# Transposing layernorm outputs and residual gradients by DMA in a two-block training step on one core

## The chip, the cores and the metric

The kernel runs on one core of a Trainium2 chip. The metric is the device time of one execution in microseconds, as the median of several runs. The core has five engines that run their own streams of instructions: TensorE (PE in the profile: matmuls, with weight loads listed as PEld), VectorE (DVE), ScalarE (ACT), GpSimd (POOL) and SyncE (SP, which here only issues DMAs). Sixteen DMA engines move the data that the queues ask for. "SPq" in a view is SP's DMA queue.

## What is computed

A forward and backward pass through four residual layers over one sequence of 2048 rows by 512 columns: linear attention (A), gated unit (B), A, B again, with the same weights in both rounds. The outputs are the result, the gradient of the input, and the gradients of the five weights.

```python
def _A_ref(x, wqkv, wo):            # 32 heads of 16
    q, k, v = ...(x @ wqkv)
    phi = lambda t: jnp.where(t > 0, t + 1, jnp.exp(t)) + 1e-6
    pq, pk = phi(q), phi(k)
    kv = jnp.einsum("bhsd,bhse->bhde", pk, v)
    z = jnp.einsum("bhsd->bhd", pk)
    o = einsum(pq, kv) / (einsum(pq, z) + 1e-6)
    return o @ wo

def _B_ref(x, w_gate, w_up, w_down):   # 512 -> 1376 -> 512
    return (sigmoid(x @ w_gate) * (x @ w_up)) @ w_down

x = x + _A_ref(_layernorm(x), A_wqkv, A_wo)
x = x + _B_ref(_layernorm(x), B_w_gate, B_w_up, B_w_down)
...                                 # both once more, then jax.vjp of all of it
```

## The kernel before, in words

The 2048 rows are 16 tiles of 128 rows (`NST`); the residual stream stays in SBUF for the whole kernel as 16 tiles `x` of 128x512 in float32. In the forward pass it holds the activations, in the backward pass the gradients. A 128x512 tile is four blocks of 128x128 (`NDC`), since a matmul sums over 128 partitions.

A scheduler orders the instructions of each engine when the program is built. It starts from the order of the source and may hoist an instruction whose inputs it thinks are ready. On each engine the order is then fixed, and every instruction waits for what it needs. All DMAs but those of the last stage are issued from SP's queue, in order. Each of them also waits for the DMA issued eight places earlier on that queue, because eight completion semaphores are used in turn.

Stages, in order of time:

- **Forward of A** (`a_fwd`, layers 0 and 2). Loop 1 takes each tile through q, k, v: three groups of four 128x512 matmuls (L468), exponentials on ACT, the rest on DVE, then a transpose of the positive feature map. Loop 2 (L521 to L546) forms the attention output and adds it to `x`. In layers 0 and 2 the transposes of the weights for the backward pass (L372, L396; one PSUM buffer for all) are emitted at tile 4 of loop 1; the scheduler spreads them.
- **Forward of B** (`b_fwd`, layers 1 and 3). Per tile 24 matmuls for gate and up (L621, L624), transposes of their product (L587), 11 matmuls for down (L599).
- **First backward pass of each layer** (`b_bwd_p1`, `a_bwd_p1`), layers 3, 2, 1, 0: from the gradient tile in `x` to the gradient of the layer's input. It saves what the weight gradients need to DRAM.
- **Second backward pass** (`b_bwd_p2`, `a_bwd_p2`): weight gradients, matmuls over all 16 tiles (L833, L863, L885), partly placed between the first passes by the scheduler.

The places that the change touches:

*Layernorm tiles in the forward pass.* Class `FwdLN` prepares one tile at a time. `stage` normalizes `x[st]` into a bf16 slice of `hstage` (statistics on DVE, power on POOL, scaling on ACT at L310), saves four tiles at once to DRAM (L426), and makes `hT`, the four transposed blocks, which the matmuls of L468, L621 and L624 use as weights. `hT` is made by `transpose_blocks`: four TensorE transposes into a PSUM tile `ln_tp` (L318), then one copy to SBUF on DVE (L325). `ensure(st + 1)` at L460 and L609 keeps it one tile ahead. The first `NPRE` = 2 tiles of the next layer are prepared at the end of the layer before (L547, L602).

*Gradient tiles in the first backward passes.* Class `GPrep`, `prep(st)`: in layer 3 the gradient is loaded from the input into `gstage` and copied to `x` (L669, L671); in the other layers `x[st]` is cast to bf16 into `gstage` on POOL (L676) and saved, two tiles at a time (L678). Then `gT`, its four transposed blocks, is made in the same way through the PSUM tile `gT_ps`, with the copy on ACT (L327). It feeds L760 in layers 3 and 1, and L958 in layers 2 and 0. `prep` is called at the top of each tile's work (L749, L948). Beside it stand the loads of what the forward pass saved: `ssd`, `h`, `o`, `pq` (L751, L696).

At the start of the kernel SP loads the input and the weights in the order x, `wqkv`, `wo`, `wg`, `wu`, `wd` (L98 to L168), with the last of x in between.

## Time and profile before

| | |
|---|---|
| median of 3 timed runs | 1394.78 us (1393.33 to 1395.5) |
| profiled execution: span from first to last instruction | 1393.1 us |
| mean granted TensorE clock | 0.988 |
| q/k/v loops (first to last L468) | 19.7 to 309.9 us, layers 0 and 2 |
| gate/up (first to last L621) | 114.8 to 475.9 us, layers 1 and 3 |
| first backward pass, B (first to last L760) | 489.5 to 1018.6 us, layers 3 and 1 |
| first backward pass, A (first to last L958) | 650.2 to 1131.4 us, layers 2 and 0 |
| end of the span | weight gradients alone |

The profile is of one execution; its page lists no other time of that execution than the span. Of the engines it lists the time in which they were busy. Matmuls are pipelined and the ends of their intervals are modelled, so the price of a matmul in a full stream is read from the starts of two neighbours and not from its listed length. In a table of stages each row is a stretch of the span with each engine's busy time. In a line of a group, the number after the first bar is the busy time of all its instructions and the mean of one in ns; after the second bar stands the engine's idle time just before them and what ended it.

### The profile page before, as it was taken

Reading aid. Unit: us, or ns where it says so; the run is one execution under the profiler, and the core shown is the slowest. Engines: PE = TensorE matmul, PEld = TensorE weight load, DVE = VectorE, ACT = ScalarE, POOL = GpSimd, SP = SyncE. Lnnn points to the kernel's source line nnn. Section 1 sums busy time; section 2 is a strip of 40 time slices with the busy share of each in tenths; the row PEclk is TensorE's granted clock in tenths of the full one; section 3 lists DMA queues with packets and bytes.
Section 4 is the critical chain, followed back from the end, with each engine's and each line's share of the span. In section 5 each row is a group of like instructions: output and inputs, shape, how many; then the busy total and the mean of one; then the engine's idle time right before and its main releaser. Section 6 shows DMA issues by size and latency. Waiting matters only on the chain. (4 is left out here: it accounts for less than half of the span.)

```text
span 1393.1 us, 25045 instructions
## 1 busy us (share of the span) xinstructions
PE 1297.9 (93%) x9956; PEld 790.1 (57%) x9956; DVE 679.9 (49%) x1468; ACT 647.3 (46%) x1168; POOL 250.5 (18%) x413
## 2 busy tenths in 40 slices
PE   4989899998899898998999999999999999988988
PEld 2555455556455444554665677555548675556767
DVE  6664644567533355665857400456640676611111
ACT  5857576775776544443547411444431447600000
POOL 4026654105633300002100100010010101100000
PEclk9999999999999999999999999999999999999999
DMA  7622334452543497547774586964568956499745
GB/s 273 230 103 103 149 152 158 147 177 98 201 178 143 169 326 259 175 168 237 218 230 148 181 227 149 334 217 167 172 199 248 275 169 192 143 311 261 175 122 162
DMA packets 268853, 269.77 MB, mean 194 GB/s; under 512 B 24576, under 2 KB 245184, under 8 KB 268736
## 3 DMA queue, kind: packets, MB, share of 16 engines
q1 hardware_dynamic: 246272, 253.50, 57.2%
q10 hardware_dynamic: 22464, 14.68, 3.6%
q8 instruction: 78, 1.28, 0.4%
q14 instruction: 39, 0.32, 0.1%
HBM read 144.57 MB, written 123.57 MB: 192 GB/s over the span
## 5 line engine op out<-in xcount | busy, mean ns | idle before, releaser
L730 ACT COPY ddT<-T_ps 128x1024 bf16<-128x1024 bf16 (+1 forms) x96 | 83.1, 867 | 103.4 <-PE T_ps L728 103.3
L630 POOL TENSOR_TENSOR ssd_t<-hh_t,oms 128x512 bf16<-128x512 bf16 (+1 forms) x96 | 100.6, 1052 | 83.0 <-ACT oms L628 48.4
L648 DVE SCALAR_TENSOR_TENSOR junk<-t_sb,h_ld 128x512 bf16<-128x512 f32 x64 | 46.1, 720 | 137.6 <-ACT t_sb L646 136.6
L762 DVE TENSOR_TENSOR dd_t<-dhh_ps,ssd_ld 128x512 bf16<-128x512 f32 (+1 forms) x96 | 60.4, 629 | 102.0 <-PE dhh_ps L760 102.0
L742 PEld LDWEIGHTS <-ddT 128*128 128x128 bf16 (+1 forms) x704 | 66.3, 98 | 71.4 <-issue 12.5
L468 PE MATMUL mm_ps<-wqkv,hT 128*128 128x512 bf16 x384 | 100.2, 386 | 0.5 <-DVE x_108 L601 0.4
L742 PE MATMUL dh_ps<-wuT,ddT 128*128 128x512 bf16 (+1 forms) x352 | 96.5, 382 | 3.9 <-ACT t_sb L646 0.9
L833 PE MATMUL p_ps<-p_set,p_a_15354 128*128 128x256 bf16 (+1 forms) x768 | 82.5, 267 | 10.8 <-DVE dw_stg L798 10.8
L629 DVE TENSOR_TENSOR hh_t<-u_ps,ssd_t 128x512 bf16<-128x512 f32 (+1 forms) x96 | 60.7, 634 | 65.3 <-PE u_ps L624 50.3
L760 PE MATMUL dhh_ps<-wdT,gT 128*128 128x512 bf16 (+1 forms) x384 | 87.8, 364 | 5.0 <-DMA wdT<-wdT_d 4.3
L624 PE MATMUL u_ps<-wu,hT 128*128 128x512 bf16 (+1 forms) x384 | 92.4, 361 | 0.0
L621 PE MATMUL g_ps<-wg,hT 128*128 128x512 bf16 (+1 forms) x384 | 92.0, 361 | 0.4 <-DVE ostage L530 0.4
L833 PE MATMUL p_ps<-p_set,p_a_10151 128*128 128x256 bf16 (+1 forms) x768 | 81.5, 261 | 0.9 <-DMA p_set<-sv_hdd_130 0.9
L599 PE MATMUL y_ps<-wd,hhT 128*128 128x512 bf16 (+1 forms) x352 | 81.4, 380 | 0.0
L742 PE MATMUL dh_ps<-wgT,ddT 128*128 128x512 bf16 (+1 forms) x352 | 81.3, 379 | 0.0
L833 PEld LDWEIGHTS <-p_a_15354 128*128 128x128 bf16 x768 | 68.9, 100 | 21.7 <-issue 8.4
L590 ACT COPY hhT<-hhT_ps 128x512 bf16<-128x512 bf16 (+1 forms) x96 | 49.5, 515 | 58.3 <-PE hhT_ps L587 58.1
L728 PEld LDWEIGHTS <-dd_t 128*128 128x128 bf16 (+1 forms) x704 | 50.7, 101 | 40.8 <-DVE dd_t L762 18.5
L833 PEld LDWEIGHTS <-p_a_10151 128*128 128x128 bf16 x768 | 67.2, 98 | 9.2
L728 PE MATMUL T_ps<-ident,dd_t 128*128 128x128 bf16 (+1 forms) x704 | 66.4, 221 | 3.6 <-DVE dd_t L762 3.5
L838 DVE TENSOR_TENSOR dw_stg<-p_ps,dw_stg 128x512 bf16<-128x512 f32 (+1 forms) x36 | 23.4, 653 | 87.5 <-PE p_ps L833 74.4
L1038 PE MATMUL dh_ps<-wqkvT,dkvT 128*128 128x512 bf16 x256 | 65.6, 380 | 0.0
(493 smaller groups left out, 2498.3 us busy)
## 6 DMA issues: line engine op xcount, KB each, us to landing
p_set<-sv_hdd_130 SPq DMA_DIRECT2D x15, 1024.0 KB, 7.1
p_set<-sv_hdd_119 SPq DMA_DIRECT2D x15, 1024.0 KB, 6.3
sv_ssd_118<-ssd_t SPq DMA_DIRECT2D x16, 688.0 KB, 3.1
sv_ssd_129<-ssd_t SPq DMA_DIRECT2D x16, 688.0 KB, 3.1
ssd_ld<-sv_ssd_129 SPq DMA_DIRECT2D x16, 688.0 KB, 5.5
sv_hdd_130<-dd_t SPq DMA_DIRECT2D x16, 688.0 KB, 3.9
ssd_ld<-sv_ssd_118 SPq DMA_DIRECT2D x16, 688.0 KB, 6.0
sv_hdd_119<-dd_t SPq DMA_DIRECT2D x16, 688.0 KB, 3.7
```

The costliest lines, as they stand in the source:

```text
L468: nc.tensor.matmul(ps[:], lhsT=hT[:, kc, :], rhs=k.wqkv[:, kc, n * D:(n + 1) * D], start=(kc == 0), stop=(kc == NDC - 1))
L599: nc.tensor.matmul(y_ps[:], lhsT=T["hhT"][0:r, fc, :], rhs=k.wd[0:r, fc, :], start=(fc == 0), stop=(fc == NFC - 1))
L621: nc.tensor.matmul(g_ps[:, 0:w], lhsT=hT[:, kc, :], rhs=k.wg[:, kc, c0:c0 + w], start=(kc == 0), stop=(kc == NDC - 1))
L624: nc.tensor.matmul(u_ps[:, 0:w], lhsT=hT[:, kc, :], rhs=k.wu[:, kc, c0:c0 + w], start=(kc == 0), stop=(kc == NDC - 1))
L629: nc.vector.tensor_tensor(hh_t[:, c0:c0 + w], u_ps[:, 0:w], ssd_t[:, 0, c0:c0 + w], ALU.mult)
L630: nc.gpsimd.tensor_tensor(ssd_t[:, 1, c0:c0 + w], hh_t[:, c0:c0 + w], oms[:, 0:w], ALU.mult)
L728: nc.tensor.transpose(tps[0:r, a, i, :], dd[:, a, fc * P:fc * P + r], k.ident[:])
L730: nc.scalar.copy(ddT[:, :, fcs[0]:fcs[0] + nfull, :], tps[:, :, 0:nfull, :])
L742: nc.tensor.matmul(dh_ps[:], lhsT=T["ddT"][0:r, a, fc, :], rhs=wT[0:r, fc, :], start=(i == 0), stop=(i == n_mm - 1))
L760: nc.tensor.matmul(dhh_ps[:, 0:w], lhsT=gT[:, jc, :], rhs=k.wdT[:, jc, c0:c0 + w], start=(jc == 0), stop=(jc == NDC - 1))
L833: nc.tensor.matmul(psv[:, icl, :], lhsT=lhs_all[:, st, ic * P:(ic + 1) * P], rhs=set_t[:, st, 0:W], start=(st == 0), stop=(st == NST - 1))
L1038: nc.tensor.matmul(dh_ps[:], lhsT=lhsT, rhs=k.wqkvT[:, n * NDC + c, :], start=(i == 0), stop=(i == 3 * NDC - 1))
```

## The change

Both uses of `transpose_blocks` in the two classes are replaced by a DMA that transposes from SBUF to SBUF, issued on SP's queue. The PSUM tiles `ln_tp` and `gT_ps` and the copies that empty them are no longer used there. `hT` gets 7 buffers in place of 4, `gT` 4 in place of 2. Layernorm tiles are prepared three tiles ahead in place of one, and 4 in place of 2 at the end of the layer before. Gradient tiles, so far prepared when they were needed, are prepared two tiles ahead by a new method `get`. All other transposes stay on TensorE.

```diff
-                hT=lctx.enter_context(tc.tile_pool(name="ln_hT", bufs=4)),
+                hT=lctx.enter_context(tc.tile_pool(name="ln_hT", bufs=7)),
...
-NPRE = 2
+NPRE = 4
...
         hT = R["hT"].tile([P, NDC, P], BF16, name="hT")
-        transpose_blocks(k, R["ps"], hT[:], [h_t[:, c * P:(c + 1) * P] for c in range(NDC)], "vector", tag="ln_tp")
+        nc.sync.dma_start_transpose(out=hT[:], in_=h_t)
...
-                ln.ensure(st + 1)
+                ln.ensure(st + 3)
...
-            ln.ensure(st + 1)
+            ln.ensure(st + 3)
...
+        self.done, self.ready = 0, {}
...
-        gT = self.work.tile([P, NDC, P], BF16, name="gT")
-        transpose_blocks(k, self.ps_tp, gT[:], [g_bf[:, c * P:(c + 1) * P] for c in range(NDC)], "scalar",
-                         tag="gT_ps")
+        gT = self.stg.tile([P, NDC, P], BF16, name="gT", bufs=4)
+        nc.sync.dma_start_transpose(out=gT[:], in_=g_bf)
         return g_bf, gT
+
+    def get(self, st):
+        while self.done <= min(st + 2, NST - 1):
+            self.ready[self.done] = self.prep(self.done)
+            self.done += 1
+        return self.ready.pop(st)
...
-            g_bf, gT = gp.prep(st)
+            g_bf, gT = gp.get(st)
...
-                g_bf, gT = gp.prep(st)
+                g_bf, gT = gp.get(st)
```

In the compiled program PE's stream begins with nine groups of four weight transposes (L372 on `wg`), and the first L468 follows them; before, it began with the transposes of two layernorm tiles and then L468. On SP's queue the first transposing DMAs stand right behind the loads of the weights. In the text below, line numbers are those of the kernel before; in the changed kernel the transposing DMAs are at L428 (hT) and L681 (gT).

## The prediction

> **What bounds the kernel now.** I read the page's busy times first, then the busy slices, then the table of stages, and last single groups.
>
> ```profile
> span 1393.1 us, 25045 instructions
> ...
> PE 1297.9 (93%) x9956; PEld 790.1 (57%) x9956; DVE 679.9 (49%) x1468; ACT 647.3 (46%) x1168; POOL 250.5 (18%) x413
> ...
> PEclk9999999999999999999999999999999999999999
> DMA  7622334452543497547774586964568956499745
> ```
>
> PE is busy 93% of the span at a nearly full granted clock, no other engine reaches half, and the DMA engines are six tenths busy. So TensorE's stream of instructions is the bound, and an instruction taken from it shortens the kernel unless something else becomes late. The chain of waits that ended last holds only the final weight gradients, a stage without any of the changed transposes. Its stalls (DMA loads of earlier partial sums, some 30 us between 1222 and 1260 us) I leave as they are.
>
> The table of stages says how much room the DMA engines have where the new transfers fall (columns: stretch, its length, busy time and count of PE, weight loads, DVE, ACT, POOL; granted clock, DMA share, GB/s):
>
> ```profile
> 18.00:72.00 54.00, 52.68 (x380) 28.46 (x379) 36.95 (x90) 45.47 (x81) 5.83 (x15) 1.00 0.69 238
> 275.00:318.00 43.00, 41.50 (x371) 24.50 (x369) 25.94 (x60) 29.33 (x54) 0.00 (x0) 0.96 0.53 181
> 645.00:700.00 55.00, 49.68 (x459) 32.36 (x457) 44.75 (x104) 26.89 (x46) 9.77 (x18) 1.00 0.76 227
> 1050.00:1135.00 85.00, 84.46 (x778) 63.86 (x777) 42.78 (x100) 31.19 (x53) 6.00 (x10) 1.00 0.82 238
> ```
>
> These four are the attention stages: q/k/v of layers 0 and 2, first backward loops of layers 2 and 0. A tile there takes 3 to 5 us, and the DMA engines are free for 54x0.31 = 16.7 us, 20.2, 13.2 and 15.3 us. With about 15, 12, 16 and 16 tiles in them that is 1.1, 1.7, 0.83 and 0.96 us of all sixteen engines per tile. The GLU stages have far more: 115 to 275 us has a DMA share of 0.38, 350 to 480 us 0.45, 480 to 645 us 0.67 and 850 to 1020 us 0.64, so 99, 72, 54 and 61 us free for 16 tiles each.
>
> **What goes.** A transpose is listed at 219 ns, but matmuls overlap, so I read the price from starts, in the timeline of PE (start, length, operation):
>
> ```profile
> 24.61 0.39 PE L318 MATMUL ln_tp<-ident,hstage 128*128 128x128 bf16 x4
> 24.84 1.46 PE L468 MATMUL mm_ps<-wqkv,hT 128*128 128x512 bf16 x6
> ```
>
> Four transposes begin at 24.61 us and the next matmul at 24.84 us: 0.23 us of the stream per tile, not 4x0.219 = 0.88. The same step stands at 27.65 to 27.88 us, and at 203.35 to 203.58 us in layer 1. There are 64 layernorm tiles and 64 gradient tiles, so 128x0.228 = **29.2 us** leave PE. This is the whole prize: 2.1% of the span.
>
> ```profile
> L327 ACT COPY gT<-gT_ps 128x512 bf16<-128x512 bf16 x64 | 37.7, 590 | 31.5 <-PE do_ps L958 15.6 <-PE gT_ps L318 11.2 <-DMA woT<-woT_d 4.4
> L318 PE MATMUL ln_tp<-ident,hstage 128*128 128x128 bf16 x256 | 26.5, 222 | 23.2 <-ACT hstage L310 21.6 <-DVE hT L325 1.6
> L325 DVE COPY hT<-ln_tp 128x512 bf16<-128x512 bf16 x64 | 26.4, 412 | 1.1 <-PE ln_tp L318 1.1
> L318 PE MATMUL gT_ps<-ident,gstage 128*128 128x128 bf16 x256 | 25.8, 219 | 6.7 <-ACT gT L327 4.0 <-POOL gstage L676 1.5 <-ACT hhT L592 0.6
> ```
>
> The evictions go too: 26.4 us on DVE and 37.7 us on ACT. Neither bounds a stage (at most ACT with 45.47 of 54 us), so I price them at nothing. PE sat idle 23.2 us ahead of the layernorm transposes, 17.9 of it the kernel's start, and 6.7 ahead of the gradient's. Of these 5.3+6.7 = 12 us at most vanish. Most lie where a stage begins and a new wait will stand there, so I take 4 us.
>
> **What comes.** 128 transposing DMAs of 128 KB, all on SP's queue. The trace has none, so I bound them. Time on the engines: the run moved 269.77 MB in a busy share of 0.613, which is 316 GB/s, so 128 KB at that rate is 0.41 us. One packet took 0.613x1393.1x16/268853 = 51 ns on average; if every row of 128 elements is a packet, 512 of them on 16 engines take 1.6 us. The far end is the row of the largest transfers with short runs, p_set, 7.1 us. From issue to landing: 128 KB rows show 2.4 to 3.0 us, p_set again 7.1. SP's own issue: from 0.32 us to 6.13 us (the one of L168 behind the weight loads). I take 0.5 us of engine time, 3 us to landing and 0.5 us of SP, the values of the rows with the same 128 to 256 KB; both ends stay for the range.
>
> At 0.5 us the transfers fit the free 0.83 to 1.7 us per tile, and cost nothing. Three tiles ahead in the q/k/v loop are 3x2.8 = 8.4 us, two ahead in the first backward loop of attention 6 to 10 us, and in the GLU loops (7.9 us per forward tile) over 15 us: enough for 3 us. If that cover goes, each tile waits for the difference. The Trainium skill's DMA: Bandwidth & Descriptors (Latency and other measured facts) has a transposing DMA measured at 261 GB/s: by that 128 KB are 0.50 us, an estimate, and the sum would stay. The skill speaks against the change too: VectorE: DVE Perf Modes (The three transpose paths) gives 390 ns for a 128x128 transpose on TensorE and 1309 ns by DMA. The row above shows four on TensorE for 0.23 us of the stream; four by DMA one after the other would be an estimated 5.2 us of the engines, and the sum would end near 1675 us. No run shows yet which holds.
>
> Each transposition waits on SP: for ACT's layernorm or POOL's cast, for PE to give a buffer back (7 and 4), and, by the order of instructions, for the DMA eight issues earlier on SP, as every DMA there does in turn. Behind it stand the saves of q, k, v and, in the backward, the loads of ssd, o and pq, for which DVE (L762, L961) and then PE wait. SP spends most of its time waiting for others, 178.5 us for DVE's hh_t at L637 alone, so 128x0.5 = 64 us more on it find room.
>
> **What moves: the start.** Before, PE begins at 17.86 us and the first L468 at 19.67 us. The order of the changed program puts nine groups of weight transposes (L372 on wg) ahead of the first L468. wg lands at 11.93+7.2 = 19.1 us. A group shares one PSUM buffer with the next, and in the trace two follow each other in no less than 0.90 us (33.98, 34.88 us), so nine end near 27.5 us. The first hT is no earlier: SP is held by L168 until 19.96 us, and its queue carries wd, which lands at 13.04+14.1 = 27.1 us. So L468 starts near 28 us, 8.5 us late, with 9x0.228 = 2 us of work already done: **+6.5 us**. Bounds: 0 if the loop catches up in its former idle time (1.3 us in 18 to 72 us says it hardly can), +12 if hT lands a further 5 us late.
>
> The two attention backwards begin with a cast on POOL and the transposition of tile 0. There 0.23+0.59 us on PE and ACT become some 3 us of DMA: **+2 us each**, with the matmuls of L863 and L885 as partial cover; +7 each if a landing is 7.1 us. The GLU backwards have gradients loaded early (layer 3) or L833 matmuls ahead of them (layer 1): 0.
>
> Sum: -29.2-4+6.5+4 = -22.7, so 1393.1 becomes 1370.4 us. The timed median 1394.78 us is 1.7 us above the profile's span, which makes **1372 us**, 1.6% less.
>
> **The rivals.**
> 1. *The DMA engines become the bound of the attention stages* (slower). For it: DMA shares of 0.69 to 0.82 there and an unknown price. Against it: 128 KB at the measured 316 GB/s is small. At T us per transposition the excess is 15(T-1.1)+16(T-0.83)+16(T-0.96), plus 12(T-1.7) above 1.7. It eats the 22.7 us at T = 1.44 us; from there on the kernel is slower. At 1.6 us the excess is 30 us: 1402 us. At 7.1 us it is 353 us there and 15+42+60+53 = 170 us in the GLU stages: near 1895 us. A transposition that holds SP's queue for T instead acts alike, with a tile's 3 to 5 us as the room. At 5 us the two q/k/v loops would lose 32x2.2 = 70 us and the attention backwards about 60: 1372+130 = 1502 us.
> 2. *A wash.* Transposes leave PE but every stage begins with a late landing: start +12, attention backwards 2x7, and no idle time gained: -29.2+12+14 = -3.2, so 1392 us. Against it: PE has other matmuls at those places.
> 3. *The change does not shorten PE's stream.* Excluded: the order of the changed program has 512 transposes and 512 weight loads fewer on PE, nothing in their place.
>
> **Numbers.** Forecast 0.48, its own range 1360 to 1386 us; rival 1 0.40, of which 0.15 lies above 1500 us; rival 2 0.09, from 1386 to 1396 us; more gain than the range 0.03. The range is 1358 to 1500 us. A measurement of this kernel can tell about 0.2% (2.8 us) from no change: faster by more than that 0.48+0.03+0.03 = 0.54, within it 0.05, slower 0.41.
>
> **What would show it.** In the profile after: PE near 1269 us busy (1297.9-29.2) with 9444 matmuls; no ln_tp, gT_ps; the q/k/v loop at some 2.8 us a tile with no PE wait for DMA hT; the rows of DMA issues with hT and gT landing in 2 to 4 us; DMA share up by 0.05; first L468 near 28 us. I am wrong if PE waits for hT or gT by DMA in every tile, if SP's issues of L428 and L681 last microseconds, or if DVE waits for ssd, o or pq loads that stand behind a transposition.

## The result

The changed kernel takes 1407.86 us (median of 4 runs, 1404.15 to 1411.94), the one before 1395.14 us on the same chip: ratio 1.0093, 95% interval 1.0072 to 1.0115. It is slower by 12.7 us, where 1372 us had been forecast. The profiled execution has a span of 1405.6 us, 12.5 us more than the 1393.1 us of before.

The head of the page of the changed kernel (busy time, share and count of each engine; granted clock and DMA share in 40 slices):

```profile
span 1405.6 us, 24154 instructions
...
PE 1280.7 (91%) x9444; PEld 762.3 (54%) x9444; DVE 653.5 (46%) x1404; ACT 615.1 (44%) x1104; POOL 249.9 (18%) x413
...
PEclk9999999999999999999999999999989989998999
DMA  9834555564764599559973886996478976499735
```

PE has the 512 matmuls fewer, DVE and ACT are freer too, and still the end comes later. The clock row is the first hint: in three slices of the second half PE is granted less than 0.9 of its clock, where before there was none.

I took the steps from one matmul's start to the next, gave each its median at full clock by width (216 ns for 512 columns, 56 for 128) as work, and called what is left a stall if over 300 ns and a small loss if under:

| us | before | after | difference |
|---|---|---|---|
| ahead of the first matmul | 17.9 | 19.4 | +1.5 |
| work | 1233.6 | 1204.9 | -28.7 |
| stalls | 80.7 | 109.5 | +28.8 |
| small losses | 56.9 | 67.8 | +10.9 |
| time at half clock | 36.3 | 75.9 | +39.6 |

The first four rows add up to the 12.5 us; the last row is no fifth term. It counts the time in which the granted clock was 0.5, which shows as small losses where PE was busy meanwhile. So the work left PE as predicted, and as much came back as stalls. Where, is read from a few marks in PE's stream (first and last matmul of an operation; "layer 2" is the stretch from the first do_ps to the first dpk_ps, "layer 0" from the first to the last do_ps, "GLU" from the first to the last dhh_ps; in the backward stretches some weight gradients run in between):

| us | before | after |
|---|---|---|
| first L468 | 19.7 | 31.1 |
| end of the forward (last u_ps) | 476.5 | 476.7 |
| GLU backward of layers 3 and 1 | 143.5, 140.8 | 132.9, 134.4 |
| attention backward, layer 2 | 58.9 | 69.3 |
| attention backward, layer 0 | 92.0 | 106.3 |

The forward ends level although 64x0.228 = 14.6 us of PE's work left it. The GLU backwards gain 17 us; 5.4 of them are 25 weight gradient matmuls (p_ps, 216 ns each) that ran inside these stretches before and run elsewhere now. The two attention backwards lose 10.4+14.3 = 24.7 us. The table of stages of the changed kernel for the four attention stages (columns as in the prediction):

```profile
31.00:85.00 54.00, 52.86 (x323) 25.50 (x320) 28.82 (x56) 43.66 (x79) 0.00 (x0) 1.00 0.70 206
260.00:313.00 53.00, 52.38 (x340) 25.89 (x338) 30.37 (x60) 43.99 (x79) 0.78 (x2) 1.00 0.59 179
640.00:709.00 69.00, 54.69 (x472) 36.22 (x471) 50.69 (x127) 22.56 (x36) 7.54 (x12) 0.93 0.98 235
1037.00:1143.00 106.00, 92.77 (x782) 68.19 (x780) 45.77 (x108) 24.83 (x40) 6.17 (x10) 0.92 0.89 239
```

The q/k/v stages keep PE full at clock 1.00. In layer 2's backward the DMA share rises from 0.76 to 0.98 while PE is busy 54.69 of 69 us, and the clock falls below 1. What PE and DVE wait for (engine, line, tile, releaser: us in total, times, longest; the first list is PE's over the span, the second DVE's from 636 to 710 us):

```profile
PE hhT_ps L587 <- DVE hh_t L629: 11.9, 8, 4.0
...
PE dnT_ps L986 <- DVE ddpad L982: 8.0, 5, 3.9
...
PE p_ps L839 <- DMA p_a<-sv_h: 6.1, 1, 6.1
PE dnT_ps L985 <- DVE dnA L974: 5.3, 2, 3.6
```

```profile
DVE dphq L990 <- DMA pq_ld<-sv_pq: 6.2, 4, 2.5
DVE prod L967 <- DMA pq_ld<-sv_pq: 5.3, 1, 5.3
```

PE waits for DVE, and DVE for the load pq_ld: 20.7 and 5.3 us in the whole span, 0.9 before. For gT itself PE waits once, 0.5 us; for hT never. POOL's cast waits 32.2 us in this stretch for a transposition that still reads its staging tile, but PE waits for no cast. SP's queue shows why the loads are late (start, length, operation):

```profile
638.87 0.58 SPq L702 DMA_DIRECT2D o_ld<-sv_o  x1
639.50 0.47 SPq L702 DMA_DIRECT2D pq_ld<-sv_pq  x1
640.07 0.41 SPq L679 DMA_DIRECT2D sv_gbf<-gstage  x1
640.52 2.76 SPq L681 DMA_TRANSPOSE gT<-gstage  x2
643.33 0.58 SPq L702 DMA_DIRECT2D o_ld<-sv_o  x1
```

In these 5 us SP issues with no pause over 0.1 us, and a transposition takes it 1.19 us at the least (median 1.21 for hT, 1.22 for gT, up to 4.67), where a plain DMA takes 0.3 to 0.6. In sum the 128 issues held SP 189.7 us. The transfers land in 2.4 to 9.4 us (median 2.5 for hT, 4.1 for gT) and took (0.654x1405.6-0.572x1393.1)/128 = 0.96 us of all 16 engines each, by the share of SP's queue. Not all of an issue's time is its own: the longest in layer 2's stretch, 4.65 us at 665.82 us, stands right behind that of a 1 MB p_set, and in the kernel before a plain issue 1.9 us behind a p_set took 2.07 us.

### The profile page after: what moved, and what is told of

Same layout as the page of the kernel before. It is cut to its first block, busy times and chain, and to the rows that moved or that the text cites. A ratio compares the mean times of both kernels' runs of the same rounds, so it can differ in the third digit from the quotient of the medians.

```text
span 1405.6 us, 24154 instructions
## 1 busy us (share of the span) xinstructions
PE 1280.7 (91%) x9444; PEld 762.3 (54%) x9444; DVE 653.5 (46%) x1404; ACT 615.1 (44%) x1104; POOL 249.9 (18%) x413
## 2 busy tenths in 40 slices
DMA packets 338482, 286.51 MB, mean 204 GB/s; under 512 B 94208, under 2 KB 314816, under 8 KB 338368
## 3 DMA queue, kind: packets, MB, share of 16 engines
q8 instruction: 74, 1.21, 0.4%
## 4 chain that ended last, share of the span: by engine, by line
PE 68%; DMA 11%; ACT 8%; DVE 4%; issue 3%; POOL 3%; SPq 1%; ACTq 0%; POOLq 0%; DVEq 0%
PE p_ps L839 14%; PE dh_ps L748 9%; PE y_ps L599 5%; PE dhh_ps L766 5%; PE g_ps L621 4%; PE u_ps L624 4%; PE p_ps L869 4%; PE mm_ps L468 4%; PE T_ps L734 3%; PE dh_ps L1044 3%; ACT pkvT L1035 2%; DMA gT<-gstage 2%; DMA pq_ld<-sv_pq 2%; DMA p_set<-sv_hdd 2%; PE do_ps L964 1%
## 5 line engine op out<-in xcount | busy, mean ns | idle before, releaser
L839 PE MATMUL p_ps<-p_set,p_a 128*128 128x256 bf16 (+1 forms) x1920 | 210.7, 270 | 20.4 <-DVE dw_stg L804 9.8
L839 PEld LDWEIGHTS <-p_a 128*128 128x128 bf16 x1920 | 176.6, 100 | 47.0 <-issue 11.8
L748 PE MATMUL dh_ps<-wuT,ddT 128*128 128x512 bf16 (+1 forms) x352 | 100.4, 381 | 0.4 <-ACT t_sb L646 0.4
L748 PEld LDWEIGHTS <-ddT 128*128 128x128 bf16 (+1 forms) x704 | 65.3, 98 | 59.3 <-issue 0.4
L468 PE MATMUL mm_ps<-wqkv,hT 128*128 128x512 bf16 x384 | 95.2, 384 | 0.6 <-DVE x L601 0.6
L650 POOL TENSOR_SCALAR ab<-c 128x2 f32<-128x2 f32 x64 | 12.3, 193 | 414.8 <-DVE junk L648 414.8
L869 PE MATMUL p_ps<-p_a,p_set 128*128 128x512 bf16 (+1 forms) x352 | 81.1, 379 | 2.3 <-DVE dw_stg L844 2.3
L646 ACT ACTIVATE t_sb<-dh_ps,rstd_all 128x512 f32<-128x512 f32 x64 | 44.0, 687 | 81.8 <-PE dh_ps L748 53.6
L734 PEld LDWEIGHTS <-dd_t 128*128 128x128 bf16 (+1 forms) x704 | 46.6, 101 | 60.3 <-DVE dd_t L768 25.4
L677 POOL TENSOR_SCALAR gstage<-x 128x512 bf16<-128x512 f32 x48 | 31.9, 686 | 247.1 <-DMA gT<-gstage 238.7
```

Of the source, the lines that this page charges most:

```text
L468: nc.tensor.matmul(ps[:], lhsT=hT[:, kc, :], rhs=k.wqkv[:, kc, n * D:(n + 1) * D], start=(kc == 0), stop=(kc == NDC - 1))
L734: nc.tensor.transpose(tps[0:r, a, i, :], dd[:, a, fc * P:fc * P + r], k.ident[:])
L748: nc.tensor.matmul(dh_ps[:], lhsT=T["ddT"][0:r, a, fc, :], rhs=wT[0:r, fc, :], start=(i == 0), stop=(i == n_mm - 1))
L839: nc.tensor.matmul(psv[:, icl, :], lhsT=lhs_all[:, st, ic * P:(ic + 1) * P], rhs=set_t[:, st, 0:W], start=(st == 0), stop=(st == NST - 1))
L869: nc.tensor.matmul(ps[0:r, :], lhsT=st_t[:, st, j * P:j * P + r], rhs=g_all[:, st, :], start=(st == 0), stop=(st == NST - 1))
```

## The experiments

Four theories were on the table. S: a transposition holds the queue that issues it, and the loads behind come late. B: the DMA engines are full there and the transfer itself costs. L: PE waits on the path cast, transposition, landing. O: the order of the work and the lookahead cost, not the DMAs. All ratios are to the kernel before on the same chip, with the 95% interval; stretches are those of the table above.

### What each half costs, and what the DMA costs

**e1_hT_only.** The changed kernel with the gradients as before.

```diff
-        gT = self.stg.tile([P, NDC, P], BF16, name="gT", bufs=4)
-        nc.sync.dma_start_transpose(out=gT[:], in_=g_bf)
+        gT = self.work.tile([P, NDC, P], BF16, name="gT")
+        transpose_blocks(k, self.ps_tp, gT[:], [g_bf[:, c * P:(c + 1) * P] for c in range(NDC)], "scalar",
+                         tag="gT_ps")
...
-            g_bf, gT = gp.get(st)
+            g_bf, gT = gp.prep(st)
```

> Layernorm outputs by DMA as in the changed kernel, gradients transposed on TensorE as before. Theory S (a transposition holds SP's queue for 1.2 us and the loads behind it in the backward come late): the forward of the changed kernel ended level with the one before (last L621 at 476.1 against 475.9 us: 14.6 us of matmuls gone, 11.4 us lost at the start, the rest in small stalls), and the backward is as before, so 1391 to 1398 us. Theory B (the transfers' 0.96 us of the 16 engines are what costs): half of the 12.7 us lost, about 1401 us. Theory O (the order and the lookahead cost, not the DMAs): 1395 to 1402 us, with the loss at the start. By all three the first L468 comes near 31 us.

**e2_gT_only.** The changed kernel with the layernorm tiles as before, their lookahead and buffers too.

```diff
-        nc.sync.dma_start_transpose(out=hT[:], in_=h_t)
+        transpose_blocks(k, R["ps"], hT[:], [h_t[:, c * P:(c + 1) * P] for c in range(NDC)], "vector", tag="ln_tp")
...
-NPRE = 4
+NPRE = 2
...
-                ln.ensure(st + 3)
+                ln.ensure(st + 1)
```

> Gradients by DMA as in the changed kernel, layernorm outputs transposed on TensorE as before. Theory S: what was lost between 476 us and the end is lost again, near 12 us, so 1403 to 1409 us, with pq_ld and p_a late between 1030 and 1060 us. Theory that the start alone lost the time: 1395-14.6 = about 1380 us. Theory B: 1401 us.

**e3_ahead_TensorE.** The changed kernel's lookaheads and buffers, both transposes on TensorE.

```diff
-        nc.sync.dma_start_transpose(out=hT[:], in_=h_t)
+        transpose_blocks(k, R["ps"], hT[:], [h_t[:, c * P:(c + 1) * P] for c in range(NDC)], "vector", tag="ln_tp")
...
-        nc.sync.dma_start_transpose(out=gT[:], in_=g_bf)
+        transpose_blocks(k, self.ps_tp, gT[:], [g_bf[:, c * P:(c + 1) * P] for c in range(NDC)], "scalar",
+                         tag="gT_ps")
```

> The changed kernel's lookahead, buffers and order of emission, with all 128 tiles transposed on TensorE as before: no transposing DMA. Theory S and theory B: within 5 us of the kernel before, 1390 to 1400 us, since the DMAs are what costs. Theory O: the new stalls (28.8 us) and the half clock behind them (11 us) come back on top of TensorE's full work: 1420 to 1435 us.

**e4_plain_copy.** The changed kernel with plain copies of the same 128 KB; the tiles are not transposed.

```diff
-        nc.sync.dma_start_transpose(out=hT[:], in_=h_t)
+        nc.sync.dma_start(out=hT[:].rearrange("p a b -> p (a b)"), in_=h_t)
...
-        nc.sync.dma_start_transpose(out=gT[:], in_=g_bf)
+        nc.sync.dma_start(out=gT[:].rearrange("p a b -> p (a b)"), in_=g_bf)
```

> The changed kernel with plain copies of the same 128 KB in place of the transposing DMAs, so the 128 tiles are not transposed; everything else is as in the changed kernel. Theory S: SP is held 0.32 to 0.5 us instead of 1.2 us per tile and the loads behind come in time: 1393-29+7 to 12 for the start, 1371 to 1385 us; q1's share falls from 65% to near 59%. Theory B, if the bytes cost and not the transposing: 1400 us or more. Theory O: 1405 to 1410 us as in the changed kernel.

| kernel | median us | ratio | end of forward | GLU 3, 1 | layer 2 | layer 0 |
|---|---|---|---|---|---|---|
| e1 hT by DMA only | 1395.69 | 1.0002 (0.9990 to 1.0013) | 475.7 | 140.9, 140.6 | 59.5 | 91.7 |
| e2 gT by DMA only | 1407.08 | 1.0078 (1.0061 to 1.0095) | 475.9 | 132.3, 133.8 | 69.5 | 103.9 |
| e3 lookahead, TensorE | 1383.33 | 0.9910 (0.9886 to 0.9933) | 485.1 | 130.2, 130.6 | 59.3 | 94.3 |
| e4 plain copies | 1380.60 | 0.9902 (0.9882 to 0.9923) | 475.0 | 131.0, 130.7 | 62.2 | 98.3 |

The whole loss is in the gradient half (e2), and the layernorm half with its late start gains nothing (e1). That the start alone lost the time is out: e2 has the old start and lost as much. The lookahead without any DMA (e3) is 12.9 us *faster* than before. That gain lies in the GLU backwards, which need 13.3 and 10.2 us less here and 7 to 13 less in e2 and e4 (2.2 and 3.2 us of it are the weight gradients that moved out). In the forward the longer lookahead on TensorE costs 8.6 us.

Transposing in place of copying the same bytes costs 1407.9-1380.6 = 27 us (ratios 1.0093 and 0.9902). This pair is the cleanest of all. The scheduler orders each engine's instructions anew for every program, so a pair can differ in its order too; this one does not. Of the 9309 matmuls recorded in e4 all but one stand in the order of the changed kernel, as do DVE's, ACT's and POOL's instructions but for one each; on SP's queue 24 of 676 DMAs stand elsewhere. So theory O falls: e4 has the changed kernel's order and is faster than before. (e3 alone does not show it, since its order differs from the changed kernel's.) Of the 27 us, 7.1 and 8.0 lie in the two attention stretches, 1.9 and 3.7 in the GLU backwards. DVE's waits for pq_ld over the whole span, first of the changed kernel, then of e4:

```profile
DVE dphq L990 <- DMA pq_ld<-sv_pq: 20.7, 8, 9.2
```

```profile
DVE dphq L990 <- DMA pq_ld<-sv_pq: 12.4, 5, 7.1
```

A plain copy took SP 0.47 us (median) and the engines (0.616x1378.7-0.572x1393.1)/128 = 0.41 us, a transposition 1.2 and 0.96.

### Where, and by which path

**e5_attn_gT_TensorE.** From the changed kernel.

```diff
-        nc.sync.dma_start_transpose(out=gT[:], in_=g_bf)
+        if self.l in (0, 2):
+            transpose_blocks(k, self.ps_tp, gT[:], [g_bf[:, c * P:(c + 1) * P] for c in range(NDC)], "scalar",
+                             tag="gT_ps")
+        else:
+            nc.sync.dma_start_transpose(out=gT[:], in_=g_bf)
```

> The changed kernel with the gradient tiles of the two attention layers (32 of the 128) transposed on TensorE again, still two ahead. Theory S, by the stretches from the first do_ps to the first dpk_ps (layer 2) and to the last do_ps (layer 0): they took 58.9 and 92.0 us before, 69.3 and 106.3 in the changed kernel, 59.3 and 94.3 with the lookahead on TensorE; they go back to 59 to 60 and 92 to 95, so about 22 us less than the changed kernel: 1383 to 1388 us. Theory B (each transposing DMA costs its share of the engines wherever it stands): a quarter of the 27 us between plain copies and transposing DMAs, so about 1400 us.

**e6_loads_first.** From the changed kernel.

```diff
-                g_bf, gT = gp.get(st)
                 o_st = old.get(st)
                 pq_st = pqld.get(st)
+                g_bf, gT = gp.get(st)
```

> The changed kernel with the o and pq loads of the attention backward written ahead of the transpositions of the same step; the number and size of the DMAs stay. Theory S: the loads no longer stand behind the transposition two tiles ahead, DVE's waits for pq_ld (20.7 us) go, and the two stretches come 10 to 20 us nearer to before: 1388 to 1398 us. Theory B, or a delay from the transposing DMA itself (its length or its share of the engines): 1404 to 1411 us, no change.

**e7_gT_from_ACT.** From the changed kernel.

```diff
-        nc.sync.dma_start_transpose(out=gT[:], in_=g_bf)
+        (nc.scalar if self.l in (0, 2) else nc.sync).dma_start_transpose(out=gT[:], in_=g_bf)
```

> The changed kernel with the gradient transpositions of the two attention layers issued from ACT's queue instead of SP's. Theory S: SP is free of 32 holds of 1.2 us and of their waits, the loads come in time, ACT takes 32 x 1.2 us in their place where it has room: 1385 to 1398 us. Theory B: the engines move the same bytes in the same way, 1403 to 1411 us.

**e9_unread.** From e5, in the branch of layers 0 and 2.

```diff
+            gT_unread = self.stg.tile([P, NDC, P], BF16, name="gT_unread", bufs=4)
+            nc.sync.dma_start_transpose(out=gT_unread[:], in_=g_bf)
```

> The kernel that lost nothing in the attention backward (gradient tiles of layers 2 and 0 on TensorE, all others by DMA, 1385.4 us) with 32 transposing DMAs added in these two layers, of the same tiles at the same places, whose result nobody reads. Theory B (the DMA engines are full there and the loads of o, pq and p_a come late): the loss of the changed kernel comes back without anything waiting for the transposition itself, 1403 to 1412 us. Theory L (PE waits on the path cast, transposition, landing, so the DMA's own length costs): nobody waits for it, 1384 to 1391 us.

**e10_gT_four_ahead.** From the changed kernel; gstage gets three buffers in place of two.

```diff
-        gT = self.stg.tile([P, NDC, P], BF16, name="gT", bufs=4)
+        gT = self.stg.tile([P, NDC, P], BF16, name="gT", bufs=6)
...
-        while self.done <= min(st + 2, NST - 1):
+        while self.done <= min(st + 4, NST - 1):
```

> The changed kernel with the gradient tiles transposed four ahead instead of two (six gT buffers, three staging buffers). Theory L: a landing of 4 us is covered, 1385 to 1392 us. Theory B: the same transfers in the same stretches, 1403 to 1411 us.

(No trace of e5 is used, hence no stretches.)

| kernel | median us | ratio | layer 2 | layer 0 |
|---|---|---|---|---|
| e5 attention's gT on TensorE | 1385.43 | 0.9925 (0.9899 to 0.9951) | - | - |
| e6 loads first | 1403.57 | 1.0061 (1.0039 to 1.0083) | 67.2 | 103.2 |
| e7 gT from ACT's queue | 1406.22 | 1.0073 (1.0048 to 1.0099) | 71.1 | 106.5 |
| e9 e5 and 32 unread transpositions | 1402.46 | 1.0062 (1.0042 to 1.0082) | 69.9 | 99.7 |
| e10 four ahead | 1410.28 | 1.0119 (1.0102 to 1.0136) | 73.0 | 104.9 |

Thirty-two of the 128 transpositions carry 22 us (e5). Theory L falls twice: more lookahead does not help (e10), and transpositions that nobody reads bring 17 of the 22 us back (e9). They do keep their source tile, so POOL's next cast waits for them, but PE's waits for a cast are 0.2 us in all of e9. Theory S, as I had it, falls too: loads ahead of the transposition of their own step win 4 us of the 10 to 20 expected (e6), and SP freed of the holds wins nothing (e7). The trace of e6 shows one reason: DVE's waits for pq_ld fell from 26.0 us to 14.4, but another load in the same queue came later, and PE's wait for p_set in layer 2's stretch rose from 1.5 to 4.4 us. What e7 did instead is in ACT's timeline of that kernel (in brackets the idle time just before and what ended it):

```profile
646.61 0.69 ACT L988 COPY dnT<-dnT_ps 128x640 bf16<-128x640 bf16 x1 [0.42 <-PE dnT_ps L986]
646.83 4.76 ACTq L681 DMA_TRANSPOSE gT<-gstage  x2
651.91 0.69 ACT L988 COPY dnT<-dnT_ps 128x640 bf16<-128x640 bf16 x1 [4.60 <-issue]
```

Two transpositions kept ACT 4.76 us, and the next dnT copy, for which PE waits, stood 4.60 us behind them. The two issues took 1.28 and 2.07 us; between them ACT's queue waited another 1.4 us, in order, before the second could go. The hold moved to another queue with something urgent in it. So e7 does not speak against a hold; it shows that the hold goes with the instruction. In layer 2's stretch PE's wait for ACT's dnT rose to 7.4 us in six places, from 2.5 in the changed kernel.

### Hold of the queue or time of the engines

From here the base is e12, the kernel before with one thing changed: gradients prepared two ahead, on TensorE. It has no transposing DMA, so a cost can be added alone, except that the scheduler may then order PE's work anew (below).

**e12_gT_ahead_TensorE.** From the kernel before; `get` is that of the changed kernel.

```diff
-        gT = self.work.tile([P, NDC, P], BF16, name="gT")
+        gT = self.stg.tile([P, NDC, P], BF16, name="gT", bufs=4)
...
-            g_bf, gT = gp.prep(st)
+            g_bf, gT = gp.get(st)
```

> The kernel before with one thing changed: gradient tiles are prepared two ahead, on TensorE as before; layernorm untouched, no transposing DMA. If the gain in the GLU backward (143.5 and 140.8 us before, 130 to 131 in every kernel with the lookahead) comes from the lookahead: forward as before (476.5 us) and the backward of the kernel with all lookaheads on TensorE (898.7 us), so 1375 to 1379 us. If it needs the transposes off PE: 1392 to 1397 us.

**e13_unread_attn.** From e12, behind the transpose of gT.

```diff
+        if self.l in (0, 2):
+            gT_unread = self.stg.tile([P, NDC, P], BF16, name="gT_unread", bufs=4)
+            nc.sync.dma_start_transpose(out=gT_unread[:], in_=g_bf)
```

> The kernel before with gradients two ahead on TensorE (1375.4 us, no transposing DMA) and 32 unread transposing DMAs added in the two attention layers' first backward loops. If the transfer itself costs there: the two stretches (59.7 and 92.8 us) grow to 66 to 70 and 98 to 104, 1388 to 1397 us. If the loss needed the other 96 transpositions too: 1375 to 1380 us.

**e14_two_plain_attn.** From e12, at the same place.

```diff
+        if self.l in (0, 2):
+            for _ in range(2):
+                gT_unread = self.stg.tile([P, NDC, P], BF16, name="gT_unread", bufs=4)
+                nc.sync.dma_start(out=gT_unread[:].rearrange("p a b -> p (a b)"), in_=g_bf)
```

> The same base with two unread plain copies of 128 KB per tile in the same places, 64 in all: 0.82 us of the 16 engines per tile by the 0.41 us that a plain copy took, against 0.96 for a transposition, and SP held about as long. If the engines' time or SP's is the cause: nearly the loss of one transposition, 1386 to 1395 us. If transposing as such is the cause (what a transposition does to the transfers beside it): 1376 to 1382 us.

**e15_unread_GLU.** From e13.

```diff
-        if self.l in (0, 2):
+        if self.l in (1, 3):
```

> The same base with 32 unread transposing DMAs in the two GLU layers' backward, where the DMA engines were 0.67 and 0.64 busy and the room was over 3 us per tile. If only full engines make a transposition cost: 1374 to 1378 us. If each costs wherever it stands: as many us as in the attention layers, 1388 us or more.

**e17_fewer_sets** from e12, **e18_fewer_sets_unread** from e13, by the same edit.

```diff
-                  sets=bctx.enter_context(tc.tile_pool(name="p2sets", bufs=3)),
+                  sets=bctx.enter_context(tc.tile_pool(name="p2sets", bufs=1)),
```

> Gradients two ahead on TensorE, no transposing DMA, and one buffer instead of three for the 1 MB sets of the weight gradients, so two p_set loads leave the middle of layer 2's attention backward loop. The weight gradients themselves wait for their sets, so the whole is slower, 1390 us or more by all theories; it is the base for the next run. The stretch from the first do_ps to the first dpk_ps stays at 59 to 61 us.

> The same with 32 unread transposing DMAs in the two attention loops. In the kernel with three sets they lengthened layer 2's stretch from 59.7 to 69.7 us. If full DMA engines are the cause: with some 14 us of transfers taken out of the stretch the growth falls to 4 us or less. If SP's hold of 1.2 us is: it stays at 8 to 11 us.

| kernel | median us | ratio | GLU 3, 1 | layer 2 | layer 0 |
|---|---|---|---|---|---|
| e12 base | 1375.35 | 0.9867 (0.9851 to 0.9883) | 131.3, 130.8 | 59.7 | 92.8 |
| e13 32 unread transpositions, attention | 1394.49 | 1.0006 (0.9994 to 1.0019) | 131.2, 130.6 | 69.7 | 98.9 |
| e14 64 unread copies, attention | 1390.62 | 0.9964 (0.9949 to 0.9980) | 130.1, 130.6 | 68.6 | 94.6 |
| e15 32 unread transpositions, GLU | 1386.66 | 0.9947 (0.9930 to 0.9963) | 138.8, 130.6 | 59.5 | 92.8 |
| e17 one set buffer | 1521.84 | 1.0915 (1.0886 to 1.0943) | - | 58.8 | 94.9 |
| e18 one set buffer and e13's DMAs | 1555.35 | 1.1155 (1.1126 to 1.1184) | - | 68.5 | 97.2 |

e13: 32 unread transpositions alone cost 19 us. e14: two plain copies per tile lengthen layer 2 by nearly as much, 8.9 against 10.0 us, but layer 0 by 1.8 against 6.1. These are the first 30 us of layer 2's stretch, first in e12, then in e14 (busy time of PE, weight loads, DVE, ACT, POOL; clock, DMA share, GB/s):

```profile
636.00:666.00 30.00, 27.37 (x249) 17.42 (x249) 24.80 (x58) 13.94 (x24) 7.23 (x12) 1.00 1.04 302
```

```profile
636.00:666.00 30.00, 22.41 (x178) 12.98 (x181) 21.35 (x48) 11.37 (x19) 6.77 (x12) 0.94 0.82 264
```

With the engines full (1.04, 302 GB/s) PE is busy 27.37 of 30 us, so full engines are not enough to make it slow. The second row seems to say that they are not needed either: with 64 small copies added they are *less* full (0.82), and PE loses 5 us. But a rival stands in it, the order of PE's work. The unread DMAs are the only edit, yet in the compiled program the scheduler placed fewer weight-gradient matmuls into layer 2's loop: between the ddpad transposes of its first and last tile stand 88 in e12, 69 in e13 and 37 in e14 (109 ns each), and of the 71 matmuls that e14 has fewer in the row above 34 are of this kind. In the first eight steps from tile to tile e12 does 35 of them in 27.6 us and e14 none in 28.5 us. So part of what PE lost there is work that e12 hides in this loop and e14 does later, and layer 2 in these runs does not separate queue from engines.

Layer 0 does compare like with like: PE's matmuls stand there in the same order in e12, e13 and e14, but for six in e14 near its start. SP's issues in its stretch add up to 31.4 us in e12, 59.6 in e13 and 60.5 in e14; the DMA shares are 0.83, 0.94 and 0.95. By both measures e13 and e14 are alike, and still 16 transpositions cost 6.1 us and 32 copies 1.8. So neither the time of SP's issues nor the fullness of the engines explains layer 0 by itself; something about transposing is not excluded. These are single profiled executions, and e13 against e14 in total is 3.9 us.

For the queue speaks that SP is what the slow kernels share in layer 2. Its issues in the 46 us from 6 us ahead of the first do_ps add up to 14.7 us before and 16.7 in e12, but 38.8 in the changed kernel, 37.2 in e13, 32.2 in e14, 36.5 in e18. e17 and e18 were meant to give the engines room: the growth of layer 2's stretch stayed (58.8 to 68.5 = 9.7 us), as the hold predicts. But with the unread DMAs the engines stood at 1.02 in the first 30 us all the same, and the count of weight-gradient matmuls in the loop fell here too (78 to 64), so by itself this pair decides little.

e15 was expected to cost nothing and cost 11 us. In layer 1 it did cost nothing (130.6), at a DMA share of 0.79. In layer 3, where the gradients are loaded from DRAM, DVE waited 10.2 us for these loads on SP's queue (1.8 in e12) and the loop grew by 7.5 us, at a share of 0.78 and in e12's order of PE's work. SP's own waits there (480 to 626 us) tell why:

```profile
SPq L685 <- DMA gstage<-in_grad_out_dram: 19.0, 6, 6.1
```

SP stood 19.0 us until a gradient had landed, because the transposition that reads it was next in order; the next gradient's load stood behind. The issues of the 12 transpositions took 15.4 us besides. So what stands behind the transposition in the queue counts, and a wait in order does as much as the issue itself. Some 6 us more were lost in the weight gradients after 772 us; a part of that is a 3.5 us wait of PE for ACT's dw_stg, the rest I have not traced.

So the loss is shown to come from transposing in place of copying (e4), 22 us of it in the attention backward (e5). Through what, is shown only in part. A transposition delays what follows it on its queue, by its issue and by its waits (e7, e15, the loads of pq); this is a mechanism of theory S, for the queue as a whole and not for single loads. How much of the 27 us it is, and how much the 0.96 us of the engines, stays open: each transposition brings both, and in e13 the engines moved 236 GB/s at a share of 1.04, in e12 302.

### Where the gain of the layernorm half went

**e8_hT_mended_gT_ahead.** From the changed kernel; gT on TensorE as in e12.

```diff
-        nc.sync.dma_start_transpose(out=hT[:], in_=h_t)
+        if l == 0 and st < 4:
+            transpose_blocks(k, R["ps"], hT[:], [h_t[:, c * P:(c + 1) * P] for c in range(NDC)], "vector", tag="ln_tp")
+        else:
+            nc.sync.dma_start_transpose(out=hT[:], in_=h_t)
```

> Layernorm outputs by DMA three ahead, but the first four tiles of layer 0 on TensorE; gradients on TensorE, two ahead. Theory S: start as before (first L468 near 19.5 us, 10 us earlier than with all tiles by DMA), so the forward ends 9 to 10 us earlier than before, and the backward is the one with the lookahead on TensorE, which took 898.7 us from the last u_ps to the end against 916.6 before: 1393-10-18 = 1365 us, between 1361 and 1371. Theory that the time lost at the start is a wait that comes back elsewhere: 1374 to 1378 us. Theory B (60 transposing DMAs at their engine cost): 1375 us or more.

**e11_nmr_on_POOL.** From e8, at L309.

```diff
-    nc.vector.tensor_scalar(nmr[:], mv[:, 0:1], -1.0, rstd_out, ALU.mult, ALU.mult)
+    nc.gpsimd.tensor_scalar(nmr[:], mv[:, 0:1], -1.0, rstd_out, ALU.mult, ALU.mult)
```

> The mended kernel (layernorm outputs by DMA but for the first four tiles, gradients on TensorE two ahead, 1374.1 us) with the layernorm's small negated product of mean and rstd computed on POOL instead of DVE. In the first GLU loop DVE waits 20.7 us in 23 places for POOL's rstd ahead of that product, with hh_t queued behind it and PE behind hh_t (7.9 us). If this wait is where the 14.6 us taken from PE in the forward went (3 us came out at its end), 3 to 6 us come back: 1368 to 1371 us. If PE's order is what costs, 1373 to 1376 us.

**e16_hT_less_ahead.** From e8, with `NPRE = 2` and five hT buffers. The first pair of lines is that of the q/k/v loop, the second that of the GLU loop.

```diff
-                ln.ensure(st + 3)
+                ln.ensure(st + 2)
...
-            ln.ensure(st + 3)
+            ln.ensure(st + 1)
```

> Gradients two ahead on TensorE, layernorm outputs by DMA but for the first four tiles, yet only two ahead in the q/k/v loops and one ahead in the GLU loops, instead of three. The lookahead of three cost the forward 9.4 us where TensorE transposes (485.1 against 475.7 us to the last u_ps). If that order of work is what ate the 13.7 us taken from PE: forward near 464 to 468 us and 1362 to 1368 us. If the forward is bound by its chain of DVE, ACT and POOL whatever the order: 1371 to 1376 us. If one ahead is too short for the landing: PE waits for hT in most tiles, 1380 us or more.

| kernel | median us | ratio | end of forward |
|---|---|---|---|
| e8 hT by DMA, start mended, gT ahead on TensorE | 1374.07 | 0.9839 (0.9811 to 0.9866) | 473.7 |
| e12 gradients ahead only, all transposes on TensorE | 1375.35 | 0.9867 (0.9851 to 0.9883) | 475.7 |
| e11 e8, small product on POOL | 1384.30 | 0.9939 (0.9919 to 0.9959) | 484.5 |
| e16 e8, less ahead | 1379.62 | 0.9894 (0.9875 to 0.9912) | 478.1 |

e8 against e12 is the layernorm half, with its longer lookahead and without the bad start: 60x4x0.056 = 13.4 us of work leave PE (1233.6 to 1220.1 by the steps) and its stalls grow by 11.5 (62.2 to 73.7). Their intervals overlap. Against e3, which has e8's lookahead and backward and transposes on TensorE, e8 does gain: its forward ends 11.4 us earlier (473.7 against 485.1) and its ratio is 0.9839 against 0.9910, 10 us. So at this lookahead most of the work taken from PE comes back as time; the lookahead had cost about as much beforehand (e3 against e12, 9.4 us). The waits of the forward, 17 to 476 us, first of e12, then of e8 (whose lines are 3 higher):

```profile
DVE ln_nmr L309 <- POOL rstd_all L307: 19.5, 23, 1.6
...
PE hhT_ps L587 <- DVE hh_t L629: 6.6, 3, 4.0
```

```profile
DVE ln_nmr L309 <- POOL rstd_all L307: 32.9, 38, 2.1
...
PE hhT_ps L590 <- DVE hh_t L632: 11.9, 8, 4.0
```

DVE's queue waits more often for POOL's rstd, hh_t stands behind it, and PE behind hh_t. I took this for the cause and moved the small product to POOL (e11). That was 10 us slower: DVE's wait for POOL moved from the product to the residual add ahead of the statistics (22.8 us), and PE waited 14.6 us for ACT's y_sb, where it was 1.8. With less lookahead (e16) the first GLU loop (first g_ps to last u_ps) took 132.8 us as in e12 and the second 135.5 against 129.8, so a shorter lookahead with the DMA did not keep the gain. The forward's GLU loops seem to be held by the chain over DVE, ACT and POOL about as much as by PE's stream; this is argued from the waits, and which link of it would have to give way is open.

## Why the prediction was wrong

**Where the forecast missed.** By parts of the profile, with the terms of the sum laid where they belong (the -4 us of stalls had no place of their own): the forward was forecast at -14.6+6.5 = -8.1 us and measured +0.2; the GLU backward -7.3, measured -17.1; the attention backward -7.3+4 = -3.3, measured +24.7; the rest 0, measured some +5. The step that failed is the price of what comes in the attention backward: "At 0.5 us the transfers fit the free 0.83 to 1.7 us per tile, and cost nothing", with 64 us more on SP that "find room". With the order of all other work kept, transposing in place of copying cost 27 us (e4).

**PE's stream.** Predicted -29.2 us, measured -28.7: right in size. That an instruction taken from PE "shortens the kernel unless something else becomes late" held only in places. I read a 93% busy PE over the whole span as the bound of each stage. In the forward 13.4 us of work gave 10 us at an equal lookahead (e8 against e3), but 1.3 us, within the uncertainty, against the kernel with the old one (e12). In the GLU backward plain copies in place of TensorE's transposes gave nothing over the lookahead alone (131.0 and 130.7 us in e4, 130.2 and 130.6 in e3).

**Stalls that vanish.** Predicted -4 us. The lookahead of the gradients alone took 18.5 us of stalls away (80.7 to 62.2, e12), and 1375.4 us is its time. I had priced the lookahead only as cover for the landing, not as a change of its own, though the gradients' lookahead is what pays most here.

**SP.** "128x0.5 = 64 us more on it find room": an issue cost 1.2 us at the least and 1.5 on average, 189.7 us in all, and in the attention backward SP had 14.7 of 46 us taken already and waits in order for buffers besides. The two +2 us for these stages measured +10.4 and +14.3. Two of the signs of an error that I had named are the ones seen: DVE waits for pq loads behind a transposition, and issues of microseconds.

**Engine time.** Taken at 0.5 us, measured at 0.96, inside the bounds of 0.41 and 1.6. The Trainium skill, Advanced Engine Details and Errata (X-Bar Transpose (TRN2)), has transposing DMAs as fast as regular ones; here 0.96 us stand against 0.41 for the copy of the same bytes, and the measurement decides. The 0.50 us estimated from DMA: Bandwidth & Descriptors was half of what was measured.

**Rival 1** has the right side and stage. Its formula for full engines gives at T = 0.96 only 16x(0.96-0.83) = 2 us, far from 24.7. Its second form, a hold of SP's queue, is seen at work, though not shown to be the whole. But I gave it "a tile's 3 to 5 us as the room", as if SP's queue held nothing else and never waited; by that a hold of 1.2 us costs nothing.

**The start.** Predicted L468 at 28 us, +6.5 net; measured 31.1. After two first steps of 2.63 and 1.57 us the nine groups followed each other at 1.10 to 1.26 us, not 0.90: each waits for the eviction of the one before, on DVE and ACT in turn, and PE's matmuls stepped at half their later pace (427 ns for 512 columns against 216; the profile records no granted clock before 34.6 us):

```profile
22.02 0.58 PE L372 MATMUL wt_ps<-ident,wg 128*128 128x128 bf16 x4 [2.02 <-DVE wt_st L353]
23.59 0.58 PE L372 MATMUL wt_ps<-ident,wg 128*128 128x128 bf16 x4 [1.00 <-ACT wt_st L355]
...
31.05 2.34 PE L468 MATMUL mm_ps<-wqkv,hT 128*128 128x512 bf16 x5
```

Most of it was regained: mending the start (e8) brings the end of the forward forward by only 476.7-473.7 = 3 us.

**Landing and cover.** 3 us taken, 2.5 and 4.1 measured; the lookahead covers it, as forecast. The q/k/v loop of layer 2 became 53.0 us for 16 tiles, 3.3 us a tile, not 2.8; it had been 55.3.

**The clock** had no term. Time at half clock doubled; at half speed 39.6 us more of it are at most 19.8 us of lost work, and the small losses grew by 11. The Trainium skill, TensorE: Matmul & The Clock Gate (What's actually happening), states a fall to half rate after an idle window of about 3.4 us. The trace agrees in kind: stalls of 3.6, 6.1 and 3.9 us at 644, 1047 and 1125 us lie beside stretches of 6.8, 10.2 and 6.8 us at clock 0.5. A stall of 2.96 us at 898.6 us had one of 3.4 too.

## What to carry to other kernels

Price a moved transpose by the queue that issues its DMA as well as by the engines: add up that queue's issues in the tightest stage, and look at what the new one waits for and what stands behind it in order. When a change brings a lookahead with it, run the lookahead alone: here it was worth 1.3% without any DMA, and transposing DMAs beside it gained nothing that can be told from noise (e8) or lost up to 2% (e13's 19 us are 1.4%, the changed kernel against e12 is 1.0093/0.9867 = 1.023). A PE that is 93% busy over the span is not the bound of every loop; the check is a stage from which PE's work is taken away. And before a probe's time is read, compare the order of the instructions in the two compiled programs: a DMA that nobody reads moved 51 of PE's matmuls out of a loop here.

## What the runs showed that was not expected

- Issuing a transposing DMA of 128x512 bf16 from SBUF to SBUF holds its queue 1.19 us or more, on SP (median 1.2) and on ACT alike (median 1.25); a plain copy of the same tile 0.47.
- It moves as some 544 packets ((338482-268853)/128) and takes 0.96 us of all 16 engines, 131 KB/0.96 us = 137 GB/s; the plain copy 0.41 us.
- In layer 2's loop the DMA engines at a share of 1.04 left PE 91% busy (e12). 64 more small DMAs made the same engines less busy and PE slower (e14), with fewer of PE's matmuls ordered into the loop.
